# A gated mix of a long convolution and a two-layer network on one core: the front half replanned with another cost model, its start reordered, and small work moved to GpSimd

## The chip, the cores and the metric

The kernel runs on one core of a Trainium2 chip. The core has five engines that run their own instruction queues side by side: TensorE (PE, matmuls), VectorE (DVE), ScalarE (ACT), GpSimd (POOL) and SyncE (SP, which only issues transfers here). PEld is the loading of weights into PE, which runs beside its matmuls. Transfers between the chip's memory and the on-chip memory are made by 16 DMA engines. The metric is the device time of one execution in microseconds, the median of several runs.

## The reference

One input `u` (2048 positions by 512 channels) goes through two branches, and a gate per position mixes them:

```python
g = sigmoid((u * gate_w).sum(-1, keepdims=True))
# branch a: a state-space convolution along the 2048 positions
dt = exp(log_dt)
K = einsum("dn,dnl,dn->dl", C, exp(dt * A * l), dt * B).real   # 512 channels, 128 states, 2048 taps
a = irfft(rfft(u, 4096) * rfft(K, 4096))[:2048] + u * Dskip
# branch b: a dense network, 512 -> 1792 -> 512
b = gelu(u @ w1 + b1) @ w2 + b2
out = g * a + (1 - g) * b
```

`A`, `B`, `C` are complex and differ for each channel and state.

## The kernel before

The program has a front (function `front`) and a tail (`conv`). In the front three streams of work share the engines.

- **Dense** (`dense`, `hidden`, `output`). The 2048 positions are handled in eight blocks of 256, and the 14 tiles of w1 and w2 in two halves of seven, so there are 16 passes `b` of 7 tiles each, cut into steps `i = 4b + j` with two tiles (one for j = 3). Every product is made in three matmuls from a high and a low part of each operand: `wh`, `xh`, `hh` hold the operand rounded to fp32r, `wl`, `xlo`, `hl` the rest. The rounding is a cast and the rest a subtraction (`split`). A hidden group is 12 matmuls of 128x256 into a bank `ph`, then ACT's gelu (L932) and cast to `hh` (L935), then DVE's subtraction to `hl` (L945), then 3 matmuls of 128x512 per tile and half block into `acc` (L965 to L967).
- **Taps** (`taps`). K is built for 16 groups of 32 channels: ACT makes exponentials and sines, DVE multiplies them up (`phases`, `magnitudes`, `rotate`, `powers`), and PE contracts them in 64 matmuls, two halves of 32, into the bank `pk` (`contract`, L693). Each pair of groups then passes a first Fourier stage of 8 matmuls (`first_stage`, L415) and goes to DRAM as `tk_d`. Parameters come for 128 channels at a time (`prepare`): `pr` holds six of them, `dtb` holds exp(log_dt) on all partitions. dt is made in `make_dt` on a 128x4 tile, written to DRAM and read back as `dtb`.
- **Signal** (`signal`). Eight first stages of `u` itself, written to DRAM as `tu_d`.

The tail reads `tu_d` and `tk_d` back, multiplies the spectra, transforms back, and adds both branches (L1129 to L1289).

**What sets the order.** The streams only list tasks: an engine, a length, a due time, and what is read and written. `Plan.run` then plays them through on a model of the engines, always giving a free engine the ready task with the smallest due time, and the instructions are issued in that order. Every engine works its own list strictly in that order on the chip, and waits where a semaphore is not there yet. The due times come from about forty constants (`T_0`, `T_MLP`, `D_KA`, ...) at the head of the file. A transfer on SP or POOL stands in the same kind of list.

**Filling matmuls.** `busy` (L386) multiplies a tile of zeros, `nil`, where PE would wait: 4 and 5 matmuls in `hidden`, 5 in `output`, 6 and 4 in the second signal stage. `warm` (L1026) makes 13 matmuls on the tile `dm` at the very start.

At the start, the 14 weight tiles of the first half come into rooms of `sk` and `y` that the taps need later; ACT casts them (three are cast by DVE, `W_DVE`) and DVE makes the low parts (L792, L790, L794).

Of the kernel before, what the change touches and what calls it, by code (L numbers as in the profile page):

```python
# [17 lines left out]
P = 128  # L18
L = 2048
D = 512  # L20
# [13 lines left out]
T_0 = 22.7  # L34
T_MLP = 411.78
K_0 = 24.88
T_KG = 373.15
U_0 = -15.83
U_GAP = 12.75
LAG = 12.23  # L40
TABLE = 9.03
D_KA = -63.09
D_KP = 0.01
D_S1 = 19.39
D_EV = -65.14
D_H = -60.13
D_LO = -10.68
PS = (2, 3, 1, 2)
N_ACC, N_H, N_PK, N_PU = PS
D_SP = 2.63  # L50
MEM = (6, 2, 3)
N_LD, N_HL, N_ST = MEM
D_XS = -33.08
D_G = 1.83
N_WARM = 13
T_EARLY, T_LOFT, T_DEN = 376.87, 422.84, 432.0
Y_K, Y_U = 41.11, 36.03
W_MLP = (-0.0634, -0.0326, 0.0273)
W_KG = (-0.0624, -0.0351, -0.0316)
W_U = (-0.058, -0.1265, 0.0001)  # L60
D_MAG = 0.58
D_ROT = 1.16
D_CON = 0.62
D_PHA = 0.72
D_PRE = 0.04
D_XL = -26.72
D_COE = 0.25
D_OUT = -5.37
N_REST = 3
FILL_H, FILL_O, FILL_U = (4, 5), 5, (6, 4)  # L70
# [7 lines left out]
W_DVE = ((1, 0), (3, 0), (5, 0))  # L78
# [94 lines left out]
class Task:  # L173
    def __init__(self, n, part, hold, done, due, table, fn, deps):
        self.n, self.part, self.hold, self.done = n, part, hold, done
# [29 lines left out]
class Plan:  # L205
# [5 lines left out]
    def add(self, part, hold, fn, due, reads=(), writes=(), table=None, done=None, after=(), rows=1.0):  # L211
        deps = set(after)
        for k in reads:
            if k in self.writer:
                deps.add(self.writer[k])
# [4 lines left out]
        t = Task(len(self.tasks), part, hold, hold if done is None else done, due, table, fn, deps)  # L220
        t.rows = rows
# [10 lines left out]
    def run(self):  # L232
        clock = Clock()
        free = dict.fromkeys(("PE", "ACT", "DVE", "POOL", "SP", "GP"), 0.0)
        ready = {p: [] for p in free}
        for t in self.tasks:
            if not t.left:
                ready[t.part].append(t)
        table, order, dma = None, [], 0.0
        for _ in self.tasks:  # L240
            best = None
            for p, ts in ready.items():
                if ts:
                    at = max(free[p], min(t.ready for t in ts))
                    if best is None or at < best[0]:
                        best = at, p
            at, p = best

            def key(t):
                return t.due + (TABLE if t.table and t.table != table else 0.0), t.n  # L250

            t = min((t for t in ready[p] if t.ready <= at), key=key)
            ready[p].remove(t)
            hold = clock.run(at, t.hold, t.rows) if p == "PE" else t.hold
            if t.table and t.table != table:
                table, hold = t.table, hold + 1.28
            free[p] = at + hold
            t.at = at
            end = at + hold
            if p in ("SP", "GP"):  # L260
                dma = max(dma, at + 1.2) + t.done
                end = dma + 0.9
            t.end = end
            order.append(t)
            for u in t.users:
                u.left -= 1
                u.ready = max(u.ready, end + WAIT.get((p, u.part), 0.13))
                if not u.left:
                    ready[u.part].append(u)
        self.end = max(free.values())  # L270
# [5 lines left out]
def gated_mix(  # L276
# [41 lines left out]
    def front(pool, psum, keep, attic, loft, den):  # L318
# [6 lines left out]
        def vec(n, fn, due, reads=(), writes=(), fast=1):  # L325

            return pl.add("DVE", 0.07 + n / 960.0 / fast, fn, due, reads, writes)

        def act(n, fn, due, reads=(), writes=(), table=None, ops=1):

            return pl.add("ACT", 0.1 * ops + n / 1200.0, fn, due, reads, writes, table)

        def mm(hold, fn, due, reads=(), writes=(), rows=1.0):

            return pl.add("PE", hold, fn, due, reads, writes, rows=rows)

        def move(kb, fn, due, reads=(), writes=(), queue="SP", after=()):

            hold = 0.45 if queue == "SP" else 1.0
            return pl.add(queue, hold, fn, due, reads, writes, done=kb / 360.0, after=after)  # L340
# [18 lines left out]
        ti = pool.tile([P, UW], I32, name="ti")  # L359
# [19 lines left out]
        nil = pool.tile([P, P], F32, name="nil")  # L379
        nc.gpsimd.memset(nil, 0.0)  # L380

        def busy(n, bank=None):

            to = acc[0][:, 0:P] if bank is None else bank[:, 0:P]
            for _ in range(n):
                nc.tensor.matmul(to, nil, nil, start=bank is not None, stop=bank is not None)  # L386
# [14 lines left out]
        def first_stage(xs, due, evac, ahead=2, fill=(0, 0)):  # L401
# [5 lines left out]
            def products():  # L407

                busy(fill[0])
                for r, (bank, _) in enumerate(banks):  # L410
                    if r == 2:
                        busy(fill[1])
# [4 lines left out]
            mm(1.2, products, due + D_S1, [*(key for _, key in xs), "c1"], [key for _, key in banks], 0.5)  # L417
# [5 lines left out]
        def signal():  # L423
            for s in range(8):
# [6 lines left out]
                def evac(r, pp, key, s=s, t=t):  # L431
                    k = take("st", N_ST)
                    act(512, lambda: nc.scalar.copy(st[k], pp), t + D_EV, [key], [("st", k)])  # L433
                    for m in range(2):
                        move(
                            128, lambda m=m: nc.sync.dma_start(rows[:, 8 * s + 4 * m + r], st[k][64 * m : 64 * m + 64]),
                            t, [("st", k)], [("u_d", 8 * s + 4 * m + r)],
                        )

                first_stage(xs, t, evac, fill=FILL_U if s == 1 else (0, 0))  # L440
# [23 lines left out]
        def make_dt():  # L464

            x, k, r, ki = dts
            ki = ki.bitcast(I32)
            ln2h = 355.0 / 512.0
            v = nc.vector
# [9 lines left out]
            def behind():  # L479
# [5 lines left out]
                v.tensor_mul(r, r, ki.bitcast(F32))  # L485

# [883 lines left out]
```

## Time and profile before

| | |
|---|---|
| median of three runs | 528.49 us (527.34 to 529.82) |
| the profiled execution, first to last instruction | 526.5 us |
| PE busy | 509.1 us |
| DVE busy | 428.4 us |
| ACT busy | 353.0 us |
| POOL busy | 41.6 us |
| first matmul of the dense branch | 6.79 us |
| first contraction of the taps | 66.18 us |
| first matmul of the tail | 418.29 us |

Rows of a timeline give the start, the duration, the engine, the line, what is written from what, the number of instructions merged into the row (x4), and in brackets the idle time of the engine just before and what ended it. The matmuls on plain fp32 (L693, L415, L386, L1026 and the tail's) show twice in the counts. Matmuls overlap, so the time that one costs is read from the start of one to the start of the next, not from its duration. Rows of windows give for each engine the busy time in that stretch.

### The profile page before, as it was taken

The page shows a single profiled execution, that of the slowest core. Times are in us where ns is not written, and L with a number is a line of the kernel's source. Part 1 is how long each engine was busy: PE and PEld are TensorE (multiplying, and loading weights), DVE is VectorE, ACT ScalarE, POOL GpSimd, SP SyncE. Part 2 cuts the span into 40 slices and gives each one's busy share as a digit, 9 for nine tenths or more (in the row PEclk, how much of TensorE's full clock was granted, in tenths as well). Part 3 has the DMA queues.
Part 4 walks back from the last instruction along what each step waited for, and adds up shares of the span by engine and source line. Part 5 has one row for each costly group of instructions (what it writes and reads, how often), then busy time and mean ns, then how long its engine had stood idle before and what let it go on. Part 6 is the DMA issues. An engine that isn't in the chain of part 4 may idle for free.

```text
span 526.5 us, 12296 instructions
## 1 busy us (share of the span) xinstructions
PE 509.1 (97%) x4858; PEld 387.8 (74%) x4858; DVE 428.4 (81%) x808; ACT 353.0 (67%) x614; POOL 41.6 (8%) x80
## 2 busy tenths in 40 slices
PE   8887999999999999999999999999999999999995
PEld 7656789898889978976988998988988722222551
DVE  6898899999999968879999989999901188777543
ACT  4989946699875689986595998456534545565311
POOL 2000000000000000000012001202010100110123
PEclk9999999999999999999999999999999999999998
DMA  8999664152685434392879026625669899999978
GB/s 241 369 301 285 222 223 153 67 202 54 159 224 201 142 91 132 111 300 86 220 156 301 3 81 126 159 40 121 201 202 172 226 309 319 366 347 375 301 277 329
DMA packets 82517, 107.87 MB, mean 205 GB/s; under 512 B 39334, under 2 KB 43562, under 8 KB 81916
## 3 DMA queue, kind: packets, MB, share of 16 engines
q1 hardware_dynamic: 76476, 85.04, 50.8%
q0 software_dynamic: 5056, 18.65, 14.0%
q10 hardware_dynamic: 928, 3.41, 1.8%
q8 instruction: 38, 0.62, 0.5%
q14 instruction: 19, 0.16, 0.1%
HBM read 61.46 MB, written 45.62 MB: 203 GB/s over the span
## 4 chain that ended last, share of the span: by engine, by line
PE 75%; ACT 11%; DMA 8%; DVE 3%; issue 2%; SPq 1%; ACTq 0%; DVEq 0%
PE pk L693 10%; PE ph L915 8%; PE ph L917 8%; PE ph L916 8%; PE acc L965 8%; PE acc L967 7%; PE acc L966 7%; PE p2u L1129 6%; PE p2k L1129 5%; PE pa L1168 3%; PE pb L1273 3%; DMA tu_d<-attic 2%; PE ph L415 2%; ACT L932 2%; ACT ph L932 2%
## 5 line engine op out<-in xcount | busy, mean ns | idle before, releaser
L915 PE MATMUL ph<-xh,wh 128*128 128x256 f32 x448 | 128.1, 286 | 2.9 <-ACT attic L433 1.8
L917 PE MATMUL ph<-xh,wl 128*128 128x256 f32 x448 | 127.0, 284 | 0.5 <-DVE wl L794 0.4
L916 PE MATMUL ph<-xlo,wh 128*128 128x256 f32 x448 | 126.6, 283 | 0.0
L915 PEld LDWEIGHTS ph<-xh,wh 128*128 128x128 f32 x448 | 85.1, 190 | 11.9 <-issue 5.6
L916 PEld LDWEIGHTS ph<-xlo,wh 128*128 128x128 f32 x448 | 85.2, 190 | 2.0
L917 PEld LDWEIGHTS ph<-xh,wl 128*128 128x128 f32 x448 | 85.1, 190 | 1.2 <-DVE wl L794 1.2
L965 PE MATMUL acc<-wh,hh 128*128 128x512 f32 x206 | 82.9, 403 | 1.3 <-ACT hh L935 1.2
L967 PE MATMUL acc<-wh,hl 128*128 128x512 f32 x206 | 81.1, 394 | 0.4 <-DVE hl L945 0.4
L966 PE MATMUL acc<-wl,hh 128*128 128x512 f32 x206 | 80.9, 393 | 0.0
L932 ACT ACTIVATE ph<-ph,b1t 128x256 f32<-128x256 f32 x112 | 50.4, 450 | 43.3 <-PE ph L917 41.3
L945 DVE TENSOR_TENSOR hl<-ph,hh 128x512 fp32r<-128x512 f32 (+1 forms) x62 | 38.3, 618 | 31.9 <-ACT hh L935 31.6
L693 PE MATMUL pk<-y,den 128*32 128x64 f32 x2048 | 61.4, 290 | 0.0
L693 PEld LDWEIGHTS pk<-y,den 128*32 128x32 f32 x2048 | 57.2, 136 | 3.7 <-issue 1.4
L965 PEld LDWEIGHTS acc<-wh,hh 128*128 128x128 f32 x206 | 38.7, 188 | 15.9 <-issue 6.8
L967 PEld LDWEIGHTS acc<-wh,hl 128*128 128x128 f32 x206 | 38.7, 188 | 10.6 <-DVE hl L945 2.0
L655 DVE TENSOR_TENSOR y<-y,ea 128x64 f32<-128x64 f32 (+4 forms) x80 | 45.2, 566 | 0.2
L966 PEld LDWEIGHTS acc<-wl,hh 128*128 128x128 f32 x206 | 38.7, 188 | 6.5
L935 ACT CAST hh<-ph 128x512 fp32r<-128x512 f32 (+1 forms) x62 | 33.0, 533 | 8.7 <-PE acc L966 5.2
L500 DVE TENSOR_TENSOR loft<-den,zz 128x256 f32<-128x256 f32 (+2 forms) x48 | 37.2, 775 | 1.7 <-ACT den L626 1.3
L501 DVE TENSOR_TENSOR loft<-den,zz 128x256 f32<-128x256 f32 (+2 forms) x48 | 37.1, 773 | 0.0
L668 DVE TENSOR_TENSOR y<-y,loft 128x2048 f32<-128x2048 f32 x16 | 36.5, 2283 | 0.0
L1137 ACT COPY k<-p2k 128x512 f32<-128x512 f32 x32 | 18.8, 586 | 24.9 <-issue 13.1
(183 smaller groups left out, 885.2 us busy)
## 6 DMA issues: line engine op xcount, KB each, us to landing
tu_d<-attic SPq DMA_DIRECT2D x64, 128.0 KB, 3.6
tk_d<-sk SPq DMA_DIRECT2D x32, 256.0 KB, 4.7
t_d<-sa SPq DMA_DIRECT2D x32, 256.0 KB, 6.8
tk<-tk_d SPq DMA_DIRECT2D x24, 256.0 KB, 4.9
t<-t_d POOLq DMA_DIRECT2D x9, 512.0 KB, 8.3
attic<-in_xt_dram SPq DMA_DIRECT2D x16, 256.0 KB, 4.4
xh_d<-xh SPq DMA_DIRECT2D x8, 512.0 KB, 3.2
xl_d<-xlo SPq DMA_DIRECT2D x8, 512.0 KB, 4.9
```

Of the source, the lines that this page charges most:

```text
L500: vec(2 * m, lambda: vv.tensor_mul(t, a, br), due, [ka, *kb], [kt])
L655: nc.vector.tensor_mul(both(n, 64 - 3 * n, n), both(0, 64 - n, n), an)
L693: nc.tensor.matmul(pks[q][32 * j : 32 * j + 32, :, gg], x[:, r, :, ch], y[:, r, :, ch], start=(r == 0), stop=(r == 1), skip_group_check=True,)
L915: nc.tensor.matmul(p, h, xh[xk][:, d], start=(d == 0), stop=False)
L916: nc.tensor.matmul(p, h, xlo[xk][:, d], start=False, stop=False)
L917: nc.tensor.matmul(p, lo, xh[xk][:, d], start=False, stop=(d == 3))
L932: nc.scalar.activation(phs[q][:, n], phs[q][:, n], AF.Gelu_apprx_tanh, bias=b1t[:, f : f + 1])
L945: nc.vector.tensor_sub(lo, phs[q][:, 0:nf], hi.bitcast(F32))
L965: nc.tensor.matmul(a, h, wh[1][w], start=start, stop=False)
L966: nc.tensor.matmul(a, h, wl[1][w], start=False, stop=False)
L967: nc.tensor.matmul(a, l, wh[1][w], start=False, stop=(j == 3))
L1129: nc.tensor.matmul(out[64 * i : 64 * i + 64], w, x, start=True, stop=True)
```

## The change

The planner's model and all its constants are new. In the model, a task's result is now ready a latency after its end, also for a later task on the same engine; transfers have a share of the wire and at most eight are open on SP. The tasks themselves change as follows.

- All filling matmuls are gone, and the 13 matmuls of `warm` are 1.
- The first signal stage has a later due time (`U_0`, `U_GAP`).
- The first 128 values of dt are computed on all partitions at once from a broadcast load of `log_dt`, straight into `dtb` (`first_dt`). The path through DRAM remains for the other three parts. The parameter array is laid out by the host so that a part of `pr` is one run of 3 KB per partition.
- `split` can cast on GpSimd: four weight tiles of the first half (`W_CAST`), three half tiles of x (`X_CAST`), and the bias casts.
- GpSimd also makes the seven scaled angles for parts 1 to 3 (ACT before), one copy per group in `magnitudes` and the skip term in `contract` (DVE before; the skip term is now added to the copy `s` and not in `pk`).
- The first two steps of `phases` are one instruction.
- The gate is 0.5 + 0.5 tanh(x/2), from the table of functions that gelu uses, instead of a sigmoid.

```diff
-T_0 = 22.7
-T_MLP = 411.78
...
-U_0 = -15.83
-U_GAP = 12.75
...
+U_0 = 28
+U_GAP = 16
...
-N_WARM = 13
...
+N_WARM = 1
...
-FILL_H, FILL_O, FILL_U = (4, 5), 5, (6, 4)
...
+SCALED = (0, 1, 1, 1)
...
+W_CAST = (0, 0, 0, 0, 0, 2, 1, 0, 0, 2, 2, 2, 0, 0)
+X_CAST = (1, 2, 2, 2)
...
-WAIT = {("PE", "PE"): 0.0, ("PE", "ACT"): 0.2, ("PE", "DVE"): 0.2}
-WAIT.update({("DVE", "PE"): 0.25, ("ACT", "PE"): 0.25, ("SP", "SP"): 0.0, ("GP", "GP"): 0.0})
+LAT = {"PE": 0.34, "ACT": 0.145, "DVE": 0.145, "GP": 0.06}
+OUT, IN = (0.75, 0.6), (1.25, 0.6)
+LANES = 8
...
             t.at = at
-            end = at + hold
-            if p in ("SP", "GP"):
-                dma = max(dma, at + 1.2) + t.done
-                end = dma + 0.9
+            end = at + hold + t.lat
+            if t.wire:
+                took, (before, behind) = t.wire
+                wire = max(wire, at + before) + took
+                end = wire + behind
...
             for u in t.users:
                 u.left -= 1
-                u.ready = max(u.ready, end + WAIT.get((p, u.part), 0.13))
...
+                u.ready = max(u.ready, end)
...
+        def first_dt():
+
+            x, k, r, ki = (loft[:, 2048 + UW * m : 2048 + UW * m + UW] for m in range(4))
+            make_dt(
+                x, k, r, ki.bitcast(I32), "tt", D_D0,
+                lambda: nc.sync.dma_start(x, logdt[:, 0:UW].to_broadcast([P, UW])), dtb,
+            )
...
             for g0 in (0, 4):
-                mm(1.89, lambda g0=g0: products(g0), t + D_KP, ["y0", "y1", ("xc", k)], [("pk", q)])
+                mm(1.89, lambda g0=g0: products(g0), t + D_KP, ["y0", "y1", ("xc", k)], [("pk", q)], lat=0.41)
...
-        def split(h, lo, src, hk, lk, key, due, on_vector=False):
-            if on_vector:
+        def split(h, lo, src, hk, lk, key, due, where=0):
+            if where == 1:
                 vec(512, lambda: nc.vector.tensor_copy(h, src), due, [key], [hk], fast=2)
+            elif where == 2:
+                pl.add("GP", 1.27, lambda: nc.gpsimd.tensor_copy(h, src), due, [key], [hk])
...
             act(
-                16, lambda: nc.scalar.activation(gate[:, 0, ts], gs[:, ts], AF.Sigmoid), t,
...
+                16, lambda: nc.scalar.activation(gate[:, 0, ts], gs[:, ts], AF.Tanh, scale=0.5), t,
```

How this moves instructions is seen at three places. The first is PE in the third pass, around the contraction of a group of taps. L693 before and L733 now are its matmuls; L965 to L967 and L1001 to L1003 are the second layer, into the banks `acc_85` and `acc_86` of the two half blocks. Before:

```order
L966 MATMUL acc_85<-wl_136,hh_138 128x512
L967 MATMUL acc_85<-wh_122,hl_141 128x512
L693 MATMUL pk_90<-y,den 32x64 x64
L965 MATMUL acc_85<-wh_123,hh_139 128x512
L966 MATMUL acc_85<-wl_137,hh_139 128x512
L967 MATMUL acc_85<-wh_123,hl_142 128x512
```

and now:

```order
L1002 MATMUL acc_86<-wl_136,hh_138 128x512
L1003 MATMUL acc_86<-wh_122,hl_141 128x512
L733 MATMUL pk_90<-y,den 32x64 x32
L1001 MATMUL acc_85<-wh_123,hh_139 128x512
L1002 MATMUL acc_85<-wl_137,hh_139 128x512
L1003 MATMUL acc_85<-wh_123,hl_142 128x512
L733 MATMUL pk_90<-y,den 32x64 x32
L1001 MATMUL acc_86<-wh_123,hh_139 128x512
```

The 64 matmuls of a group stood together and are now two runs of 32 with other work between them. This is so in all 16 groups: 16 runs of 64 before, 32 runs of 32 now.

The second place is ACT around its first gelu, which the second layer waits for (`ph_87` and `ph_88` are the first two steps' banks, `wh_114` to `wh_123` high parts of weights). Before:

```order
L792 CAST wh_119<-sk 128x512
L792 CAST wh_114<-y 128x512
L932 ACT_TABLE_LOAD
L932 ACTIVATE ph_87<-ph_87,b1t 128x256 x2
L935 CAST hh_138<-ph_87 128x512
L792 CAST wh_120<-sk 128x512
L792 CAST wh_121<-y 128x512
```

and now:

```order
L835 CAST wh_118<-sk 128x512
L574 ACTIVATE loft<-pr 128x128 x7
L835 CAST wh_114<-y 128x512
L835 CAST wh_120<-sk 128x512
L585 ACTIVATE ea_98<-pr 128x128 x6
L585 ACTIVATE den<-pr 128x128 x5
L835 CAST wh_116<-y 128x512
L835 CAST wh_123<-y 128x512
L970 ACT_TABLE_LOAD
L970 ACTIVATE ph_87<-ph_87,b1t 128x256 x2
L973 CAST hh_138<-ph_87 128x512
L970 ACTIVATE ph_88<-ph_88,b1t 128x256 x2
```

The first gelu stood behind the casts of half of the weights, and now stands behind the last of them (`wh_123`) and behind the exponentials of the taps.

The third place is DVE ahead of the first `hl`, which the same products of the second layer need (`wl_` are low parts of weights). Before:

```order
L794 TENSOR_TENSOR wl_129<-y,wh_115 128x512
L530 TENSOR_TENSOR pr<-pr,dtb 128x512
L945 TENSOR_TENSOR hl_141<-ph_87,hh_138 128x512
L794 TENSOR_TENSOR wl_134<-sk,wh_120 128x512
L794 TENSOR_TENSOR wl_135<-y,wh_121 128x512
```

and now:

```order
L837 TENSOR_TENSOR wl_135<-y,wh_121 128x512
L593 TENSOR_TENSOR loft<-loft 128x896
L837 TENSOR_TENSOR wl_130<-y,wh_116 128x512
L837 TENSOR_TENSOR wl_136<-y,wh_122 128x512
L837 TENSOR_TENSOR wl_137<-y,wh_123 128x512
L485 TENSOR_SCALAR dts_151<-dts_150 128x4
...
L596 TENSOR_SCALAR ti<-loft 128x4x32
L696 TENSOR_TENSOR y<-y,ea_98 128x2x32
L983 TENSOR_TENSOR hl_141<-ph_87,hh_138 128x512
```

`hl_141` stood ahead of five of the 14 low parts and now stands behind all of them, and behind the first angles of the taps.

On PE, before the first contraction, stand 14 hidden groups, 70 matmuls of the second layer and three signal stages before; now 18 groups, 88 matmuls and two stages, and of these the first six groups are ahead of the second layer's first matmul (four before). After the last first stage of the taps stand 11 hidden groups and 30 matmuls of the second layer before, and 9 groups and 30 matmuls now.

More of the change, by code (lines that the diff above doesn't have):

```diff
@@ L230, in add, with run, key @@
         return t
[L232 removed]
+    def run(self, fixed=None):
         clock = Clock()
[L234 removed]
+        free = dict.fromkeys(("PE", "ACT", "DVE", "SP", "GP"), 0.75)
         ready = {p: [] for p in free}
         for t in self.tasks:
+            t.left, t.ready = len(t.deps), 0.0
             if not t.left:
                 ready[t.part].append(t)
[L239 removed]
+        heads = {p: list(ts)[::-1] for p, ts in fixed.items()} if fixed else None
+        table, order, wire, lanes = None, [], 0.0, []
+        def key(t):
+            return t.due + (TABLE if t.table and t.table != table else 0.0), t.n
         for _ in self.tasks:
@@ L266, in run @@
                 u.left -= 1
-                u.ready = max(u.ready, end + WAIT.get((p, u.part), 0.13))
-                if not u.left:
+                u.ready = max(u.ready, end)
+                if not u.left and not heads:
                     ready[u.part].append(u)
-        self.end = max(free.values())
+        self.end = max(t.end for t in order)
         self.order = order
```

300 lines of the change are left out of this document (159 added, 141 removed).

## The prediction

> **What bounds the kernel now.** I read the page's first part, then the windows, then what PE waits for, then PE's timeline.
>
> ```profile
> span 526.5 us, 12296 instructions
> PE 509.1 (97%) x4858; PEld 387.8 (74%) x4858; DVE 428.4 (81%) x808; ACT 353.0 (67%) x614; POOL 41.6 (8%) x80
> ...
> 0.00:22.00 22.00, 18.04 (x112) 15.77 (x113) 15.81 (x35) 14.01 (x25) 3.68 (x15) 1.00 0.91 299
> 22.00:62.00 40.00, 34.79 (x230) 26.14 (x229) 35.80 (x87) 37.09 (x67) 0.54 (x1) 1.00 0.93 302
> 62.00:100.00 38.00, 38.00 (x464) 32.18 (x463) 37.27 (x72) 24.80 (x42) 0.25 (x2) 1.00 0.44 140
> 383.00:418.00 35.00, 35.00 (x355) 31.75 (x354) 4.40 (x8) 14.10 (x29) 3.91 (x5) 1.00 0.81 197
> 418.00:491.00 73.00, 72.20 (x376) 20.23 (x378) 57.26 (x94) 41.56 (x79) 6.20 (x12) 1.00 0.96 337
> ...
> PE acc L967 <- DVE hl L945: 0.4, 1, 0.4
> ```
>
> In a window's row stand the busy times of PE, PEld, DVE, ACT and POOL, then PE's granted clock, the DMA share and GB/s. From 62 us to the tail PE is busy throughout, and the last row, PE's waits between 62 and 418 us, has 0.4 us in all. So the front's end is PE's work plus what PE loses in the first 62 us. There "busy" hides losses, since the filling matmuls count:
>
> ```profile
> 1.14 4.58 PE L1026 MATMUL pk<-dm 128*128 128x128 f32 x26 [1.14 <-POOL dm L1021]
> 6.79 0.39 PE L915 MATMUL ph<-xh,wh 128*128 128x256 f32 x1 [1.07 <-ACT wh L792]
> 12.12 1.05 PE L386 MATMUL ph<-nil 128*128 128x128 f32 x8
> 15.19 1.28 PE L386 MATMUL acc<-nil 128*128 128x128 f32 x10
> 17.91 0.50 PE L965 MATMUL acc<-wh,hh 128*128 128x512 f32 x1 [1.21 <-ACT hh L935]
> 19.69 0.40 PE L960 MATMUL acc<-b2r,ones 128*128 128x512 f32 x1
> 21.31 0.28 PE L915 MATMUL ph<-xh,wh 128*128 128x256 f32 x1
> 22.74 0.40 PE L965 MATMUL acc<-wh,hh 128*128 128x512 f32 x1
> 24.20 0.64 PE L415 MATMUL ph<-attic,c1t 32*64 32x512 f32 x1
> 25.28 0.50 PE L965 MATMUL acc<-wh,hh 128*128 128x512 f32 x1
> 36.11 0.39 PE L915 MATMUL ph<-xh,wh 128*128 128x256 f32 x1 [1.11 <-ACT attic L433]
> 42.55 0.64 PE L415 MATMUL pu<-attic,c1t 32*64 32x512 f32 x1 [1.95 <-ACT attic L433]
> 66.18 3.84 PE L693 MATMUL pk<-y,den 128*32 128x64 f32 x128
> ```
>
> These rows give prices, start to start: a hidden group 22.74 - 21.31 = 1.43; a matmul of the second layer (21.31 - 19.69)/7 = 0.23; a signal stage 25.28 - 24.20 = 1.08. By the order PE has done 14 groups, 70 matmuls and 3 stages when it reaches the first contraction: 20.0 + 16.1 + 3.2 = 39.3 us of work. It took from 6.79 to 66.18, 59.4 us. **20.1 us are lost** to fillers and to waits for ACT: that is what the change can win.
>
> **The change, step by step.** First, when can PE start and when does its work flow? SP's list now opens with x, not with log_dt (about 0.4 us sooner), but 64 KB of log_dt and 384 KB of `pr` stand ahead of the weights: 0.45 MB at 299 GB/s is 1.5 us. The first group, at 6.79 now, starts near 8. It makes no difference: all weights and `pr`, 4.6 MB, are the same bytes as before. What counts is the second layer's first matmul, which by the order waits for ACT's cast of the last weight and for all of DVE's low parts:
>
> ```profile
> 18.28 2.19 ACT L792 CAST wh<-y 128x512 fp32r<-128x512 f32 x4
> ...
> 16.31 0.93 ACT L932 ACTIVATE ph<-ph,b1t 128x256 f32<-128x256 f32 x2
> 17.27 0.59 ACT L935 CAST hh<-ph 128x512 fp32r<-128x512 f32 x1
> ...
> 23.33 1.28 ACT L548 ACT_TABLE_LOAD   x1
> ...
> 19.10 2.49 DVE L794 TENSOR_TENSOR wl<-y,wh 128x512 fp32r<-128x512 f32 x4
> ```
>
> The four casts ran from 18.28 without a wait, so the weights had landed by then. ACT: cast of the last weight 18.3 to 18.9, table load 1.28, gelu 0.93, `hh` 0.59: 21.7. DVE, from x near 4.0: 16 subtractions of 0.62 (2.49/4) are 9.9; ten steps of the first dt on 128 columns at about 0.25 are 2.5, where 128x4 took 0.16 (bounds 0.16 and 0.62); eight small or medium operations for bias, `pr` and angles about 4; two casts 0.9; four dt steps 0.8: near 22. So ACT and DVE meet at 22, `hl` is there at **22.3**, and PE flows from there. Before it PE has six groups ready (8.6 us) in the 14 us since 8; they end near 20.5 as their last weights are cast, so 1.8 us idle.
>
> From 22.3, by the order, 12 groups, 88 matmuls and 2 stages stand ahead of the first contraction: 17.2 + 20.2 + 2.2 = 39.6, so 61.9 without a wait. I walked ACT through its list (two sine sets, seven gelus): each `hh` comes 0 to 1 us before PE wants it. The second block's x is behind 3.1 MB after the last weight, at 302 GB/s 10.4 us, so it lands near 28, is cast on GpSimd, and PE wants it at 29.8. With so little slack I allow 2 us of waits (bounds 0 and 7, what ACT's 37.09 of 40 us in the second window leaves). First contraction: 63.9. By then PE has done 48.2 us of work, not 39.3. **Lead: 66.2 - 63.9 + 8.9 = 11.2 us.**
>
> Moving the signal stages later is inside this sum: the rows at 36.11 and 42.55 are PE waiting for ACT to clear a stage's banks, and the order now has over 6 us of other work between two stages. Fillers and `warm` are 0 for the same reason: they filled waits.
>
> Second, a loss in the steady part. The order cuts 16 contractions into 32.
>
> ```profile
> 366.51 0.28 PE L917 MATMUL ph<-xh,wl 128*128 128x256 f32 x1
> 366.72 3.83 PE L693 MATMUL pk<-y,den 128*32 128x64 f32 x128
> 370.48 0.39 PE L915 MATMUL ph<-xh,wh 128*128 128x256 f32 x1
> 370.71 0.28 PE L916 MATMUL ph<-xlo,wh 128*128 128x256 f32 x1
> ```
>
> Groups of 128x256 step by 0.12. [...] 16 more runs at 0.2 to 0.33: 3.2 to 5.2 us; I take 0.28, **4.5 us back**.
>
> Third, GpSimd. No row shows its cast. A memset of 128x512, below, writes only; a two-input addition reads twice: 0.55 and 1.27. At 1.27 the four weight casts and the bias end by about 18, before DVE asks for them, and x of the second block by 30.5, which is just in time; I price it at 0, with up to 8 us in a rival.
>
> ```profile
> 2.01 0.55 POOL L866 MEMSET attic<- 128x512 f32 x1
> ...
> 510.54 1.27 POOL L1283 TENSOR_TENSOR loft<-loft,sa 128x512 f32<-128x512 f32 x1 [0.44 <-ACT sa L1282]
> ...
> 2.42 0.31 DVE L472 TENSOR_SCALAR dts<-dts 128x4 f32<-128x4 f32 x1 [1.55 <-DMA dts<-in_logdt_dram]
> ...
> 3.93 0.16 DVE L482 TENSOR_SCALAR dts<-dts 128x4 f32<-128x4 f32 x1
> ```
>
> DVE loses per group a copy, a phase step and the skip term, some 0.17 each, 8 us over 16 groups, and GpSimd's angles take ACT's. Neither engine ended PE's waits after 62 us, so I count 0. The tanh gate saves table loads, but the order as a whole has 50 instead of 47 of them: 3.8 us of ACT, which had over 100 us free after 62. First dt: its old road ended in DVE's wait for `dtb` at 17.10; PE's first contraction was not waiting for that alone, so it is inside the sum above.
>
> Fourth, the tail. It follows the taps' last stage, which ended at 395.39:
>
> ```profile
> 395.39 0.39 PE L915 MATMUL ph<-xh,wh 128*128 128x256 f32 x1
> ...
> 397.55 9.77 SPq L735 DMA_DIRECT2D tk_d<-sk  x8
> 411.07 1.00 SPq L1110 DMA_DIRECT2D tk<-tk_d  x2
> ...
> DMA to landing us min/median/max: 2.7/4.9/8.8
> ...
> 418.29 1.08 PE L1129 MATMUL p2k<-tk,cc 128*64 128x512 f32 x4
> 420.17 1.08 PE L1129 MATMUL p2k<-tk,f 128*64 128x512 f32 x4 [0.80 <-ACT f L1118]
> ```
>
> PE had 22.9 us of work behind that stage and has 9 groups and 30 matmuls now, 19.8. The first taps were back 18.4 to 20.6 us behind it (15.7 to the read, 2.7 to 4.9 to landing), the second pair up to 3 us later. So 0 to 3 us of a wait at the tail's start; I take **1.4 us**. The rest of the tail is the same code.
>
> Sum: 526.5 - 11.2 + 4.5 + 1.4 = 521.2 for a profiled execution. The median of the runs lies 528.49 - 526.5 = 2.0 above the span: **523.2 us**.
>
> [...] The warm-up's 26 records fill 4.58 us, 0.18 each, the filler's 10 at 15.19 only 0.10 to 0.13 each: the first matmuls ran slower, and one warm matmul now leaves that to the first groups. [...]
>
> **Rivals.**
>
> *A, 523.2, as summed.*
>
> *B, more is won.* No waits between 22 and 62 (-2), a contraction's cut costs the 0.2 alone (-1.3), the second layer starts 2 us sooner as `pr` comes in rows of 3 KB. 523.2 - 5.3 = 517.9. For it: that ACT and DVE meet at 22 with nothing to spare looks planned; against: the loads ran at 299 GB/s with the DMA engines at 0.91.
>
> *C, slower: GpSimd holds DVE up.* The first row at 2.42 is a DVE operation beside the memset at 2.01 and took 0.31, its like at 3.93 with GpSimd idle 0.16. If every GpSimd cast stops DVE for its whole length, DVE's chain to `hl` grows by the five casts of bias and weights, 5 x 1.27 = 6.4, and the second block's x by 2.5; the 21 angles and 32 small operations take another 1 to 2 from a DVE that is busy 37.27 of 38 us. 523.2 + 6.4 + 2.5 + 1.5 = 533.6. It decides the sign from 5.3 us on. Against: a memset shared DVE's time for 0.15 us only, of 0.55.
>
> [...]
>
> *D, no change: the stall moves.* The second block's x, behind four more loads, lands 3 us after PE wants it, and ACT, full to 62 us, lets each `hh` slip: 7 us of waits and not 2, so 528.2. The change would then not do what it says: PE still waits, for other work.
>
> **How the numbers follow.** A 0.52, B 0.21, C 0.14, D 0.13. 0.5% is 2.6 us, about what a measurement here can tell from none: faster means below 525.9, slower above 531.1. A's own range is 519.5 to 527; about 0.07 of the chance lies over 525.9. Faster: 0.21 + 0.45 = 0.66. Same: 0.13 + 0.07 = 0.20. Slower: 0.14. The range leaves out half of C and the lower third of B: 517 to 533.
>
> **What would show it.** First product of the second layer at 21 to 23 us; first contraction near 64 us with 18 groups before it; 32 runs of L733 with 0.2 us at both ends; no PE wait over 1 us between 64 and the tail; tail's first matmul near 411.6 and 109.6 us from there to the end. Wrong if the weights' low parts on DVE end after 24 us (C), if x of the second block ends PE's waits (D), or if PE's waits after 62 us sum to more than 3 us.

## The result: slower by 1.5%

| | before | changed |
|---|---|---|
| median of the runs, measured together | 527.91 us (527.08 to 529.82) | 535.02 us (534.0 to 539.28) |
| ratio | | 1.0145 (95%: 1.0103 to 1.0188) |
| profiled execution | 526.5 us | 533.4 us |
| first contraction of the taps | 66.18 us | 68.65 us |
| first matmul of the tail | 418.29 us | 424.54 us |

The forecast was 523.2 us. Its sum for a profiled execution was 521.2, so 12.2 us have to be found. Read as before: the page's first part, then the windows (PE, PEld, DVE, ACT, POOL, granted clock, DMA share, GB/s), then PE's waits between 62 and 424 us.

```profile
span 533.4 us, 12168 instructions
...
22.00:40.00 18.00, 15.69 (x81) 13.01 (x80) 17.90 (x41) 17.60 (x26) 2.12 (x3) 0.91 0.64 231
62.00:80.00 18.00, 16.25 (x214) 13.40 (x214) 17.25 (x35) 10.20 (x21) 2.27 (x3) 1.00 0.87 301
100.00:150.00 50.00, 45.38 (x488) 38.44 (x489) 41.02 (x73) 37.51 (x63) 11.93 (x14) 0.93 0.24 73
150.00:383.00 233.00, 233.00 (x2637) 199.32 (x2639) 214.84 (x375) 176.47 (x284) 35.32 (x70) 1.00 0.56 150
...
PE ph L430 <- POOL s L751: 4.6, 1, 4.6
PE acc L1003 <- DVE hl L983: 1.8, 1, 1.8
```

Before the change PE lost 0.4 us behind 62 us, and its clock was 1.00 in all of the front's windows shown. Now there are three places where it loses: between 22 and 40 us at a clock of 0.91, near 64 us, and once between 100 and 150 us, at a clock of 0.93. The largest single wait has a new releaser: one GpSimd instruction, the skip term's addition at L751. PE's timeline shows all three, and the tail's start:

```profile
22.15 0.39 PE L996 MATMUL acc<-b2r,ones 128*128 128x512 f32 x1
23.68 0.50 PE L1001 MATMUL acc<-wh,hh 128*128 128x512 f32 x1 [1.15 <-ACT hh L973]
25.58 0.50 PE L1003 MATMUL acc<-wh,hl 128*128 128x512 f32 x1 [1.16 <-DVE hl L983]
26.46 0.63 PE L1003 MATMUL acc<-wh,hl 128*128 128x512 f32 x1
29.45 0.50 PE L1003 MATMUL acc<-wh,hl 128*128 128x512 f32 x1
...
66.11 0.49 PE L1003 MATMUL acc<-wh,hl 128*128 128x512 f32 x1 [1.75 <-DVE hl L983]
68.65 2.02 PE L733 MATMUL pk<-y,den 128*32 128x64 f32 x64
...
136.06 1.07 PE L430 MATMUL ph<-s,c1t 32*64 32x512 f32 x2
141.75 1.11 PE L430 MATMUL ph<-s,c1t 32*64 32x512 f32 x1 [4.62 <-POOL s L751]
143.69 0.80 PE L1001 MATMUL acc<-wh,hh 128*128 128x512 f32 x1
146.10 0.28 PE L953 MATMUL ph<-xh,wh 128*128 128x256 f32 x1
...
424.54 1.04 PE L1163 MATMUL p2k<-tk,cc 128*64 128x512 f32 x2 [1.62 <-ACT hh L973]
```

From 136.06 to 146.10 PE did one first stage and six second-layer matmuls: 10.0 us for 1.08 + 6 x 0.23 = 2.5 us of work. 7.6 us are lost, 4.6 of them in the wait; behind it the first matmuls of 128x512 start 0.42 to 0.59 us apart instead of 0.23. What GpSimd and VectorE did meanwhile (timelines of the changed kernel):

```profile
L751 POOL TENSOR_TENSOR s<-s,dm x16: 192/376/4732, 75.6 to 400.3; 128x8 f32<-128x8 f32 x16
...
136.97 4.73 POOL L751 TENSOR_TENSOR s<-s,dm 128x8 f32<-128x8 f32 x1 [2.13 <-ACT s L750]
...
136.55 1.22 DVE L696 TENSOR_TENSOR y<-y,ea 128x1024 f32<-128x1024 f32 x1
137.68 0.68 DVE L529 TENSOR_TENSOR loft<-x,zz 128x512 f32<-128x512 f32 x1
138.28 0.68 DVE L530 TENSOR_TENSOR loft<-x,zz 128x512 f32<-128x512 f32 x1
138.89 0.21 DVE L644 CUSTOM_DVE_ANT_0 phase<-ti 128x128 uint16<-128x128 uint16 x1
139.02 2.28 DVE L708 TENSOR_TENSOR y<-y,loft 128x2048 f32<-128x2048 f32 x1
141.22 0.41 DVE L531 TENSOR_TENSOR x<-loft 128x256 f32<-128x256 f32 x1
141.56 0.68 DVE L983 TENSOR_TENSOR hl<-ph,hh 128x512 fp32r<-128x512 f32 x1
```

The first row gives minimum, median and maximum of the 16 additions in ns: 192, 376 and 4732. The slow one began in a row of VectorE operations without a gap, each starting some 0.08 us before the former's end, and ended at 141.70, 0.07 us behind the end of L531 (141.63). By then L983 had run for 0.14 us, the first operation of the row that has an operand in PSUM, the memory that PE writes (`ph`).

### The profile page after: what moved, and what is told of

It is laid out like the page before. It is cut to its first block, busy times and chain, and to the rows that moved or that the text cites. A ratio compares the mean times of both kernels' runs of the same rounds, so it can differ in the third digit from the quotient of the medians.

```text
span 533.4 us, 12168 instructions
## 1 busy us (share of the span) xinstructions
PE 506.1 (95%) x4786; PEld 381.3 (71%) x4786; DVE 428.8 (80%) x772; ACT 349.1 (65%) x589; POOL 78.8 (15%) x141
## 4 chain that ended last, share of the span: by engine, by line
PE 78%; DVE 7%; DMA 5%; ACT 3%; issue 3%; POOL 2%; SPq 1%; DVEq 0%; ACTq 0%; POOLq 0%
PE pk L733 11%; PE ph L953 9%; PE ph L955 8%; PE ph L954 8%; PE acc L1001 8%; PE acc L1003 7%; PE acc L1002 7%; PE p2u L1163 6%; PE p2k L1163 5%; PE pa L1202 3%; PE ph L430 3%; PE pb L1307 3%; DVE wl L837 1%; DMA sk<-in_w_dram 1%; DMA t_d<-sa 1%
## 5 line engine op out<-in xcount | busy, mean ns | idle before, releaser
L953 PE MATMUL ph<-xh,wh 128*128 128x256 f32 x448 | 130.6, 291 | 7.5 <-ACT wh L835 7.5
L953 PEld LDWEIGHTS ph<-xh,wh 128*128 128x128 f32 x448 | 86.3, 193 | 20.7 <-issue 9.7
L954 PEld LDWEIGHTS ph<-xlo,wh 128*128 128x128 f32 x448 | 86.4, 193 | 2.4
L1001 PE MATMUL acc<-wh,hh 128*128 128x512 f32 x206 | 83.8, 407 | 1.1 <-ACT hh L973 1.1
L1003 PE MATMUL acc<-wh,hl 128*128 128x512 f32 x206 | 81.6, 396 | 2.9 <-DVE hl L983 2.9
L733 PE MATMUL pk<-y,den 128*32 128x64 f32 x2048 | 64.8, 291 | 0.0
L733 PEld LDWEIGHTS pk<-y,den 128*32 128x32 f32 x2048 | 56.5, 136 | 7.2 <-issue 3.2
L983 DVE TENSOR_TENSOR hl<-ph,hh 128x512 fp32r<-128x512 f32 (+1 forms) x62 | 38.1, 614 | 27.7 <-ACT hh L973 27.6
L1001 PEld LDWEIGHTS acc<-wh,hh 128*128 128x128 f32 x206 | 39.3, 191 | 15.1 <-issue 7.0
L1003 PEld LDWEIGHTS acc<-wh,hl 128*128 128x128 f32 x206 | 39.2, 190 | 12.7 <-DVE hl L983 3.8
```

The costliest lines, as they stand in the source:

```text
L733: nc.tensor.matmul(pks[q][32 * j : 32 * j + 32, :, gg], x[:, r, :, ch], y[:, r, :, ch], start=(r == 0), stop=(r == 1), skip_group_check=True,)
L953: nc.tensor.matmul(p, h, xh[xk][:, d], start=(d == 0), stop=False)
L954: nc.tensor.matmul(p, h, xlo[xk][:, d], start=False, stop=False)
L983: nc.vector.tensor_sub(lo, phs[q][:, 0:nf], hi.bitcast(F32))
L1001: nc.tensor.matmul(a, h, wh[1][w], start=start, stop=False)
L1003: nc.tensor.matmul(a, l, wh[1][w], start=False, stop=(j == 3))
```

## The experiments

Unless said otherwise, an experiment keeps the order that the changed kernel's planner gives, and only what the diff shows differs. All but the three runs beside the kernel were timed, with the kernel before on the same chip.

**The changed kernel again.** 

> The changed kernel once more, as the yardstick of the other runs. If the 4.6 us wait of PE for one GpSimd addition near 137 us is a fixed feature of the order, it is in this profile too and the time is 534 to 536 us; if it hangs on a meeting by chance of GpSimd and VectorE, it is missing or elsewhere, and the times spread over 4 us or more.

538.54 us (533.34 to 541.46), ratio 1.0176 (1.0133 to 1.0219). The same addition took 4.74 us and PE waited 4.6 us for it: a fixed feature of the order. But the times spread over 6 us even without the slowest, so a spread doesn't tell the two apart.

**One addition on VectorE.** 

> One instruction moves: the skip term of the fourth group, 128x8, goes from GpSimd to VectorE, all else in the same order. Theory S (GpSimd gets its operands only between VectorE's two-input operations, so one addition of 0.2 us took 4.7 us, PE waited 4.6 us for it and then ran some 2 us at half clock): the wait near 137 us is gone, time 5 to 7 us below the changed kernel, 528 to 530 us. Rival W (PE would wait there anyway, for the next late thing): less than 2 us below. Rival M (another addition is locked out in its place): a wait of over 2 us for GpSimd elsewhere.

```diff
-pl.add("GP", 0.25, lambda: nc.gpsimd.tensor_add(at0, at0, d0), t + D_S1, ["dm"], [key])
+pl.add("GP", 0.25, lambda: (nc.vector if g == 3 else nc.gpsimd).tensor_add(at0, at0, d0), t + D_S1, ["dm"], [key])
```

529.32 us, ratio 1.0034 (1.0011 to 1.0057). The stage and the matmul behind the six of the second layer, in this run:

```profile
136.20 1.70 PE L430 MATMUL ph<-s,c1t 32*64 32x512 f32 x3
...
139.80 0.28 PE L953 MATMUL ph<-xh,wh 128*128 128x256 f32 x1
```

One instruction of 12168 on another engine takes 5.7 us off the first measurement of the changed kernel and 9.2 off the one of the same batch. PE waits for GpSimd nowhere. The stage and the six matmuls take 3.6 us here, not 10.0, so 6.4 of the 7.6 us belong to the addition: 4.6 of waiting and 1.8 behind it, at a granted clock of 0.54 (141.75 to 146.10 in the changed kernel). The other 1.2 us the stage loses without it too.

**VectorE paused, the addition left on GpSimd.** 

> The changed kernel with one VectorE instruction more: in the fourth group VectorE copies the eight columns that GpSimd's addition writes, so that it pauses until that addition is done; the addition stays on GpSimd. Theory S (VectorE's running row shuts GpSimd out): the addition takes under 1.3 us, PE's wait for it is gone or under 1 us, and the time is that of the run with this one addition on VectorE (529.3), within 2 us. Rival N (the addition takes 4.7 us at this place by itself, for a reason of GpSimd): the addition and PE's wait stay above 4 us, VectorE waits 4 us too, and the time is 535 us or more.

```diff
+def skip():
+    nc.gpsimd.tensor_add(at0, at0, d0)
+    if g == 3:
+        nc.vector.tensor_copy(d0, at0)
```

528.06 us, ratio 1.0003 (0.9981 to 1.0025). GpSimd and VectorE around it, in this run:

```profile
138.24 0.19 POOL L753 TENSOR_TENSOR s<-s,dm 128x8 f32<-128x8 f32 x1 [2.13 <-ACT s L750]
...
137.61 0.28 DVE L532 TENSOR_TENSOR x<-den 128x128 f32<-128x128 f32 x1
138.46 0.17 DVE L755 COPY dm<-s 128x8 f32<-128x8 f32 x1 [0.56 <-POOL s L753]
138.54 1.22 DVE L696 TENSOR_TENSOR y<-y,ea 128x1024 f32<-128x1024 f32 x1
```

The same addition at the same place takes 0.19 us when VectorE stands still for 0.56 us. A slow GpSimd is ruled out: VectorE's running row held it. An added instruction that makes VectorE wait made the kernel 7 us faster. Another addition of this run, the ninth, took 3.46 us (0.92 in the changed kernel), but PE did not wait for it.

**The contraction's halves together.** 

> The two halves of each contraction stand together again, 16 runs of 64 matmuls, all else in the order of the changed kernel. By the split theory (0.28 us for each of 16 extra runs, 4.5 us in all): 3 to 5 us below the changed kernel, 530 to 532 us, the stall near 137 us still there. Rival (the split gives time to what follows, and the merged order waits for ACT or VectorE instead): within 1.5 us of the changed kernel, with new waits of PE between 68 and 424 us.

```diff
-mm(1.89, lambda g0=g0: products(g0), t + D_KP, ...
+mm(1.89, lambda g0=g0: g0 or (products(0), products(4)), t + D_KP, ...
```

541.38 us, ratio 1.0259 (1.0223 to 1.0296): both expectations missed. The waits say why:

```profile
PE ph L430 <- POOL s L751: 10.4, 2, 5.9
...
98.52 8.62 POOL L751 TENSOR_TENSOR s<-s,dm 128x8 f32<-128x8 f32 x1 [2.46 <-ACT s L750]
```

The second addition, 0.23 us at 97.12 in the changed kernel, now falls 1.4 us later into a row of VectorE operations and takes 8.62 us. A third takes 4.09 us at 278.89, where PE does not wait for it. What the merge gives is hidden behind that, so it was tried again without GpSimd's additions.

**All additions on VectorE, halves together.** 

> All 16 skip terms on VectorE and the contraction's halves together again, the rest in the order of the changed kernel. Theory S: the two waits for GpSimd that made the merged kernel slow (10.4 us) are gone, and the 2.3 us that the merge saved inside the contractions, with some 1 us at the entries behind them, show: 2 to 4 us below the run with one addition moved (529.3), 525.5 to 527.5 us. Rival (the merged order itself is bad): 529 us or more, with PE waiting for ACT or VectorE in its first stages.

525.15 us, ratio 0.9936 (0.9911 to 0.9961): faster than the kernel before. The merge and the other 15 additions together gave 529.32 - 525.15 = 4.2 us (5.2 by the ratios); this run does not tell the two apart.

**Filling matmuls.** 

> Two times ten filling matmuls of 128x256, 0.12 us each, in PE's pauses before and in the second layer's first products (22.3 to 25.6 us), all else in the same order. Clock theory (the pauses cost PE half its clock from 26.1 to 29.5 us, 12 matmuls x 0.2 = 2.4 us): granted clock 1.0 in 22 to 40 us, the first contraction 2 to 2.5 us sooner, time 1.5 to 2.5 us below the changed kernel. Rival (hidden): PE gets there sooner and then waits longer, at 64 us for VectorE's low part, which itself waits for a load: time within 1 us of the changed kernel.

```diff
+def busy(n):
+    for _ in range(n):
+        nc.tensor.matmul(acc[1][:, 0:SB], wh[0][0][:, 0:P], xh[0][:, 0], start=True, stop=True)
...
+    if (i, s) == (0, 0):
+        busy(10)
...
+    if (i, s, n) == (0, 0, 0):
+        busy(10)
```

535.55 us, against 535.02 and 538.54 without: not told apart by that spread. So the same on top of the merged kernel: 

> The run before with the 20 filling matmuls around the second layer's first products. Clock theory: 1.5 to 2.5 us below it, 523.5 to 525.5 us, faster than the kernel before the change. Rival (hidden behind the wait at 64 us): within 1 us of it.

525.20 us, ratio 0.9942 (0.9915 to 0.9968), against 525.15 without. The windows of this run:

```profile
22.00:40.00 18.00, 17.80 (x109) 15.46 (x107) 17.90 (x41) 17.60 (x26) 2.31 (x3) 1.00 0.67 240
40.00:68.00 28.00, 24.66 (x168) 19.59 (x167) 24.28 (x66) 21.89 (x38) 1.10 (x2) 1.00 0.82 264
```

The clock is 1.00, PE did what it should, and the time is the same. DVE stays at 17.90 of 18 us and ACT at 17.60. That PE's half clock (0.50 from 26.46 to 29.45 in the changed kernel) was hidden behind them is argued from this; the move below tests it.

**GpSimd's casts on VectorE.** 

> As the run with all additions on VectorE and merged halves, and GpSimd's casts (four weight tiles, three half tiles of x, two of the bias) on VectorE too, in the same places of the order. Theory S (a cast on GpSimd takes some 0.4 us from VectorE, which is what the same cast costs there, 0.43): within 1 us of it, the first low part of the second layer within 0.7 us of where it was. Rival (GpSimd's casts come for free): 1.5 to 3 us slower, as VectorE does seven casts more ahead of that low part. The third way (a cast on GpSimd stops VectorE for its whole 0.8 us): 2 us faster or more.

```diff
-pl.add("GP", 1.27, lambda: nc.gpsimd.tensor_copy(h, src), due, [key], [hk])
+pl.add("GP", 1.27, lambda: nc.vector.tensor_copy(h, src), due, [key], [hk])
...
-nc.gpsimd.tensor_copy(ones, one)
-nc.gpsimd.tensor_copy(b2r, b2f)
+nc.vector.tensor_copy(ones, one)
+nc.vector.tensor_copy(b2r, b2f)
```

524.55 us, ratio 0.9945 (0.9916 to 0.9974), and the first product of `hl` at 26.13 us instead of 26.00. Against casts on VectorE, those on GpSimd gained nothing and cost nothing.

**One VectorE operation later.** In both kernels that follow, additions are on VectorE and halves are merged. 

> The run with all additions on VectorE, merged halves and the filling matmuls, and in it one VectorE operation later: the eleventh half of the gate's dot products, which waited 1.6 us for its load near 62 us, stands behind the low part that PE waits for (and the load behind it on its ring follows it). Theory V (up to the first contraction VectorE is the bound, and PE's half clock is hidden behind it): PE's 2.2 us wait near 64 us shrinks to under 1 us, the first contraction comes 1 to 2 us sooner, and the time is 1 to 2 us below the run without the move (525.2). Rival (the wait moves on to VectorE's next product): within 0.7 us of it.

```diff
-for t in pl.run():
+order = pl.run()
+n = [k for k, t in enumerate(order) if t in held][10]
+to = [k for k, t in enumerate(order) if k > n and t in lows][0] + 1
+moved = [t for t in order[n:to] if t is order[n] or t in order[n].users]
+order[n:to] = [t for t in order[n:to] if t not in moved] + moved
+for t in order:
```

> The same move without the filling matmuls. Theory V: with the wait near 64 us gone, PE's half clock from 26 to 30 us is no longer hidden: 1 to 2 us slower than with both, and within 0.7 us of the run with neither (525.15). Rival: equal to the run with both.

523.95 us with fillers (0.9924, 0.9895 to 0.9954) and 523.16 without (0.9921, 0.989 to 0.9951). The wait near 64 us is gone in both. Rows of the first contraction, of the merged kernel, the one with fillers, with the move and fillers, and with the move alone:

```profile
70.53 3.84 PE L733 MATMUL pk<-y,den 128*32 128x64 f32 x128
```
```profile
69.34 0.89 PE L733 MATMUL pk<-y,den 128*32 128x64 f32 x24
```
```profile
68.19 1.01 PE L733 MATMUL pk<-y,den 128*32 128x64 f32 x28
```
```profile
66.27 3.83 PE L733 MATMUL pk<-y,den 128*32 128x64 f32 x128
```

The first product of `hl` stood at 26.00, 25.61, 26.76 and 25.17 us, so the way from there took 44.5, 43.7, 41.4 and 41.1 us. The move takes 2.3 and 3.4 us off that way, the fillers next to nothing, with or without the move: theory V was right that VectorE's order is the bound there, and wrong that the half clock (0.91 from 22 to 40 us without the fillers, 1.00 with them) would show once the wait was gone. In the time the move is worth 1 to 2 us by the medians and about 1 by the ratios; the intervals overlap, so that alone would not show it.

**The additions in the old order.** 

> The kernel before the change with one thing of the change alone: the 16 skip terms are added by GpSimd to the copy, behind ScalarE's copy, instead of by VectorE in the bank; the order of all else is as before. Theory S: where an addition falls into a row of VectorE operations, PE waits in the first stage; by the chance of three to five such meetings of 2 to 8 us in 16, of which PE's list shows one or two, 4 to 10 us slower than the kernel before. Rival (the waits are a feature of the new order alone): within 1.5 us of the kernel before, no wait of PE for GpSimd over 1 us.

```diff
-vec(8, lambda: nc.vector.tensor_add(at0, at0, d0), t + D_LO, ["dm"], [("pk", q)])
+vec(8, lambda: None, t + D_LO, ["dm"], [("pk", q)])
...
-act(512, lambda: nc.scalar.copy(xs, pks[q].rearrange("p s g -> p (s g)")), t + D_S1, [("pk", q)], [key])
+def out():
+    nc.scalar.copy(xs, pks[q].rearrange("p s g -> p (s g)"))
+    nc.gpsimd.tensor_add(xs[:, 504:512], xs[:, 504:512], d0)
+act(512, out, t + D_S1, [("pk", q)], [key])
```

528.99 us, ratio 1.0015 (0.9995 to 1.0036). The expected 4 to 10 us did not come: the slowest of the 16 additions took 1.76 us, and PE waited for none. In the old order GpSimd's additions cost nothing that can be measured; the new order and the addition make the stall together. Whether that is because the first stages follow later there, or because no long row meets an addition, was not taken apart.

**GpSimd beside VectorE, alone.** 

> No part of the kernel's computation, and zeros as output: GpSimd and VectorE side by side on tiles of their own. Four additions of 128x8 on GpSimd beside eight multiplications of 128x1024 with two on-chip operands; beside eight operations with one operand; beside eight subtractions with one operand in PSUM; then four casts of 128x512 on GpSimd beside twelve subtractions of 128x512 and beside twelve copies, and each alone. Theory S: beside operations with two on-chip operands an addition takes as long as one to three of them (1.2 to 4 us) and a cast holds the subtractions up by some 0.4 us each; beside operations with one operand an addition takes its 0.2 us. Rival (any VectorE operation shuts GpSimd out, or the 4.7 us were a hazard of the write to the same tile): no difference between the kinds, or 0.2 us everywhere.

> No part of the kernel's computation, and zeros as output. Three additions of 128x8 on GpSimd beside ten VectorE operations that, unlike in the last such run, write ten different tiles, so that each starts before the former ends, as in the kernel: multiplications of 128x1024 with two on-chip operands; operations with one on-chip operand; subtractions with one operand in PSUM; multiplications with one PSUM subtraction as the fifth; then four casts of 128x512 on GpSimd beside twelve subtractions. Theory F (GpSimd gets in only where VectorE pauses between two operations): the second addition takes over 5 us beside the multiplications, up to the whole row of 11.5 us, and about 4.6 us where the PSUM subtraction is the fifth. Rival B (GpSimd gets in at every boundary, and the 4.7 us in the kernel have another cause): 1.2 us, as in the last such run.

> No part of the kernel's computation, and zeros as output. GpSimd's addition of 128x8 now comes as in the kernel: alone, behind a copy of ScalarE, in the middle of a row of overlapping VectorE operations. Six rows: ten multiplications of 128x1024; the same with two additions behind each other; the kernel's complex products with a broadcast operand; ten multiplications and a cast of 128x512 instead of the addition; twelve operations with one operand; four multiplications of 128x2048. Theory C (a request that comes into a running row isn't let in before the row ends or a PSUM operand comes): 4 us or more in the first rows. Theory P (it depends on the pattern: only the broadcast products shut it out): 1.2 us in the first row, over 2 us in the third. Rival B: one operation's rest, at most 1.2 us (2.3 in the last row), in all of them, and the 4.7 us stay without a mechanism.

GpSimd and VectorE in the second of the three (three additions beside ten multiplications with two on-chip operands; three beside ten subtractions with one PSUM operand; four casts beside the first of two rows of twelve subtractions):

```profile
6.13 2.49 POOL L332 TENSOR_TENSOR small<-small,skip 128x8 f32<-128x8 f32 x3
24.44 0.52 POOL L332 TENSOR_TENSOR small<-small,skip 128x8 f32<-128x8 f32 x3
42.22 3.66 POOL L336 CAST cast<-src 128x512 fp32r<-128x512 f32 x4
...
6.21 11.44 DVE L341 TENSOR_TENSOR to<-big,big 128x1024 f32<-128x1024 f32 x10
24.59 6.06 DVE L349 TENSOR_TENSOR to<-bank,big 128x512 f32<-128x512 f32 x10
42.39 8.85 DVE L360 TENSOR_TENSOR to<-big,big 128x512 f32<-128x512 f32 x12
51.65 7.30 DVE L363 TENSOR_TENSOR to<-big,big 128x512 f32<-128x512 f32 x12
```

Beside the multiplications the first addition ran before the row, and the two others waited for the end of one operation each: 2.49 us for three. Beside PSUM subtractions three took 0.52 us, as when alone (0.68 for four, in the first of these runs). Beside operations with a single on-chip operand they were held too (1.66 us for four, in the first of these runs), so two operands are not needed for it. Four casts made twelve subtractions 8.85 - 7.30 = 1.55 us longer, 0.39 each (0.29 each in the first of these runs). Theory S held in its direction and for the casts. Theories F, C and P fell in these rows: neither the overlapping row, nor an addition that comes alone into it, nor the broadcast pattern made an addition wait for more than the running operation, at most 1.3 us. So these runs do not reproduce the 4.7 us; rival B is what they show.

## Why the prediction was wrong

The terms of the sum against what the changed kernel's profile has:

| term | predicted | measured |
|---|---|---|
| lead at the first contraction | -11.2 | 68.65 - 66.18 - 8.9 = -6.4 |
| 16 contractions cut in two | +4.5 | 3.5 |
| GpSimd | 0 | +6.4, by one addition |
| the rest of the loss at that first stage | 0 | +1.2 |
| wait at the tail's start | +1.4 | +1.6 |
| rest of the tail | 0 | 533.4 - 424.54 - 108.2 = +0.7 |
| sum, from 526.5 | 521.2 | 533.5 (profiled: 533.4) |

The third and fourth rows are the 7.6 us lost from 136.06 to 146.10, divided as the run with that addition on VectorE divides them. The second is what then remains: PE took 355.9 us from the first contraction to the tail; the work left would have taken 352.1 - 8.9 = 343.2 at the pace of before; the difference is 12.7, less 7.6 and 1.6.

**The step that failed most** is "Third, GpSimd". It priced GpSimd's small operations at 0, and one of them cost 6.4 us. The reason given was that neither DVE nor ACT ended PE's waits behind 62 us. It looked at what DVE saves and not at how long an operation takes on its new engine, which the next stage waits for. The trace of before could bound it only from one addition of 128x512 at 1.27; I took GpSimd's durations as fixed. In these runs they hang on what VectorE does: 0.19 to 4.73 us for the same 128x8. The prediction's own sign of being wrong, waits of PE after 62 us of more than 3 us in all, came: 4.6 + 1.8 + 1.6. Rival C came to 533.6, near the measured time, but by luck, with the roles reversed: it had GpSimd stop VectorE for 6.4 us of casts. At the stall VectorE stops GpSimd. Of the price that it did forecast for casts on VectorE, 2.0 us came true, which the sum had at 0; they are part of the lead, below.

In the separate runs an addition waited out the running operation (1.2 us), and operations with a PSUM operand did not hold it (0.52 us for three). Of these two engines the prediction had weighed only that GpSimd holds VectorE (rival C). A wait for one operation, as in those runs, does not give the stall: 4.73 us over six of them.

**The lead** was mis-sized by 4.8 us. "I walked ACT through its list" was the gap: DVE was walked only up to 22 us. It is busy 17.90 of the 18 us from 22 to 40, and it ends PE's waits at 25.58 (3.3 us behind the 22.3 forecast) and at 66.11. On PE's timeline that is 3.3 us of a late start, 1.75 us of a wait and seven matmuls at half clock (0.50 granted), 1.4 us: 6.4 us where 2 were allowed, 4.4 of the 4.8. Where DVE's list was eased by one operation (the move), the way to the first contraction got 2.3 to 3.4 us shorter. The 3.3 us at the start have two causes, which DVE's and GpSimd's rows of the changed kernel show:

```profile
6.79 0.23 DVE L485 TENSOR_SCALAR loft<-loft 128x128 f32<-128x128 f32 x1 [2.09 <-DMA loft<-in_logdt_dram]
16.30 1.08 DVE L837 TENSOR_TENSOR wl<-sk,wh 128x512 fp32r<-128x512 f32 x1
17.30 1.03 DVE L590 TENSOR_SCALAR loft<-loft 128x896 f32<-128x896 f32 x1
18.26 1.09 DVE L837 TENSOR_TENSOR wl<-y,wh 128x512 fp32r<-128x512 f32 x1
19.27 0.68 DVE L837 TENSOR_TENSOR wl<-sk,wh 128x512 fp32r<-128x512 f32 x1
24.84 0.68 DVE L983 TENSOR_TENSOR hl<-ph,hh 128x512 fp32r<-128x512 f32 x1
...
16.22 1.63 POOL L833 CAST wh<-y 128x512 fp32r<-128x512 f32 x2 [2.28 <-DMA y<-in_w_dram]
18.18 0.63 POOL L833 CAST wh<-y 128x512 fp32r<-128x512 f32 x1 [0.32 <-DMA y<-in_w_dram]
```

The prediction had DVE at work from 4.0 without a pause; it stood still for 2.1 us, to 6.79, for the load of log_dt. And each of GpSimd's five casts of weights and bias made an operation of DVE 0.4 us longer (a low part 1.08 instead of 0.68), 2.0 us in all; before the change, with GpSimd idle, the operation that L590 now makes in 1.03 took 0.63 (L553 at 23.34). That makes 4.1 us; as the first `hl` ended at 25.5 instead of 22.3, the rest of the walk must have been priced some 0.9 too high.

**The clock.** From 26.46 to 29.45 seven matmuls took 0.43 us each, not 0.23, at a granted clock of 0.50. Two pauses of 1.2 us with two matmuls between them came before it, and with fillers in both the clock stayed at 1.00. Such pauses do not always do it: in the run with the casts on VectorE, pauses of 1.0 and 1.29 us at the same place left the clock at 1.00. What decides between the two no run here shows. At the start, where the prediction left slower matmuls to the first groups, those of 128x256 came some 0.21 us apart from 11.08 to 16.03 and 0.12 behind that. Half clock cost no time where fillers undid it (525.20 against 525.15), and 1.8 us behind the stall at 137 us.

**What held.** The cut contractions: 3.5 us by the table, and 4.2 by the experiment that also moved 15 additions, against 4.5. Of the 0.28 us a run in that sum, the rows of before show 0.09 on entering (0.21 from 366.51 to 366.72, where a step is 0.12) and 0.11 on leaving (0.23 from 370.48 to 370.71); for the 0.08 on top, an estimate, no run shows a cause. In the changed kernel's trace the first group's two halves took 1.95 and 1.96 us from their first matmul to the next work (68.65 to 70.60, 72.21 to 74.17), and the whole group before 3.77 (66.18 to 69.95): 0.14 more. The tail's wait: 1.6 against 1.4 in size. What ended it in this profile was ACT's cast of the last hidden group; the load of `tk`, which the sum had in mind, ended it with the one addition on VectorE and with the pause (2.3 and 2.2 us). The fillers: twenty of them around the second layer's first products gained nothing; the old places were not tried.

**What stays open.** Why this addition lost against six VectorE operations in turn, and another in the merged kernel against some twelve, when in three separate runs one always got in behind the running operation. That VectorE's row holds it is shown by the pause. The kernels' traces narrow down which boundary lets it in. Seven additions took over 2 us, in five profiles (3.46 to 8.62). Six of them ended 0.14 to 0.16 us into the first VectorE operation with an operand in PSUM, as at L983 above, and the seventh 0.06 us behind the end of VectorE's row. That is theory C, which the separate rows do not show. Nor does it hold for every wait: an addition of 1.17 us at 222.93 in the changed kernel got in between two operations without one. Where the additions fell, each separate row without a gap repeats one shape, while the kernel's rows mix shapes; that was not tried. Open too is the spread of the changed kernel's times, 533 to 540 us without the slowest.

The best kernel of these runs is the change with the skip terms back on VectorE, the contractions whole, and one dot product later: 523.16 us, 0.9921 (0.989 to 0.9951) of the kernel before. That is 4.8 us less than the kernel before. By the prediction's own terms, with no contraction cut, the new order was to win 11.2 - 1.4 = 9.8; about half of that is there.

## What to carry to other kernels

Moving a small operation to an idle engine is not free because that engine is idle: ask who waits for its result and how long it can be kept waiting there, and price it beside the busiest stretch of the engine that held it here, not alone (4.73 us against 0.19). When a schedule is packed by a model, a duration that depends on the neighbour has to be in the model, or the operation has to stay where its duration is sure. And a pause, or one instruction moved, at the exact place is a far sharper test of a suspected stall than undoing a part of the change.

## What was not expected of the hardware

- A 128x8 addition on GpSimd took 0.19 us beside a still VectorE and 4.73 us beside a running one; the longest seen was 8.62 us. Six of the seven waits over 2 us ended in a VectorE operation with an operand in PSUM.
- A cast of 128x512 on GpSimd made VectorE's subtractions 0.39 us longer, about what VectorE needs to do the cast itself (0.41 to 0.43 at L831), so the cast saved VectorE nothing. In the changed kernel it was 0.4 us per cast.
- An added VectorE instruction that only waits made the kernel 7 us faster (528.06 against 535.02).
